# Early beta as rows turned on TensorE, held weight and Q/V loads, and a newly searched order, in a DeltaNet + SwiGLU kernel

## The chip, the cores and the metric

The kernel runs on one core of one Trainium2 chip. The metric is the device time of one execution in microseconds (us). A traced execution gives the profile: its span is the time from the first to the last recorded instruction, and its own time also holds what lies around the span.

## The reference

The first block is a DeltaNet with batch 4, 8 heads, 768 tokens and a head width of 48. The second is an RMS norm and a SwiGLU feed-forward on all 3072 tokens, 384 wide, with 1536 hidden columns.

```python
k_n = k / (np.linalg.norm(k, axis=-1, keepdims=True) + 1e-06)
for t in range(S):
    kt, vt, bt = k_n[:, :, t], v[:, :, t], beta[:, :, t, None]
    y[:, :, t] = einsum('bhd,bhde->bhe', q[:, :, t], state)
    v_old = einsum('bhde,bhd->bhe', state, kt)
    state = state + bt[..., None] * einsum('bhd,bhe->bhde', kt, vt - v_old)
x = y.transpose(0, 2, 1, 3).reshape(B * S, H * D)
rms = sqrt(mean(x * x, axis=-1, keepdims=True) + 1e-06)
xn = x / rms * rms_g
g = xn @ w_gate
out = (g / (1 + exp(-g)) * (xn @ w_val)) @ w_out
```

q, k, v and beta are fp32. The three weight matrices and `rms_g` lie in DRAM as fp64, two 32-bit words for a value, and the kernel makes fp32 of them.

## The kernel before

**Chunks.** The sequence goes in 12 chunks of C = 64 tokens. The 32 heads of all batches go as 16 pairs, with a pair's two heads on the two halves of the partitions. For each chunk a triangular system within the chunk is solved, which gives the updates u. The state is one 48 x 48 matrix for each head.

**The first two chunks.** Chunks 0 and 1 solve their system by blocks of 16 rows (`prep16`). Its steps on the way are: K turned on PE (L648) and its scores K K^T (L671); `shares` on DVE, which weights the squared reciprocal norms by beta into `krd`; a gather on PE (L780); a recursion on DVE; masks (L880 on DVE) and coupling products (L888 on PE) that ACT copies into ET (L893). In `recur` the first rows (L1190) then give u, and three rounds of coupling follow (L1202 on PE, with u copied out by ACT at L1244 and summed by DVE at L1250). The state update (L1284) and the output products (L1212) close the chunk. Their beta lies in `beta_0`, 64 partitions of 16 values for each half and chunk, filled by four DMAs whose pieces are single values (`load_small`).

**The later chunks.** From chunk 2 on the inverse is made in blocks of W = 32 (`prep`). K's scores are copied out by ACT and go through DRAM (`dkk`) into `at`, a layout with one system in each partition; POOL scales them by beta (L944); 15 steps of multiply and reduce on DVE (L991, L997) invert; ACT and POOL spread the inverse (L1017), and transfers carry it (`dx`, `dxt` in DRAM) into `m1bd`, `x2bd` and `mt`. On PE, `merge1` (L1046) and `merge2` (L1066) make the block below the diagonal; `mr` (L1176) multiplies the inverse into the right sides and gives u (L1246); `pu` (L1212) gives the output. `on_state` (L1105) multiplies K and Q by the state, from chunk 3 on in one group. Q's scores and transpose are in `qpart`.

**The feed-forward.** A chunk's output goes through root mean square (L1315 adds up yn on DVE, L1321 squares on ACT, L1334 takes the power on POOL), scale (L1349) and transposes (L1366) into xp, for chunk 1, and xf. Chunks 0 and 1 use plain products (`ffn_plain`, L1433 up and L1415 down). The rest use a fast matrix multiplication with 15 products for the first layer (L1526) and 7 for the second (L1583), whose weights are sums formed once (`factors`, `out_factors`).

**Weights.** `weights(n0, n1)` loads and converts 18 pieces of 768 KB. Each is loaded into one of three raw buffers, pieces n = 3 and 4 into two early buffers that lie in `hf`, the feed-forward's hidden tile, whose first use for that comes later. Conversion of a piece is one step on ACT (L588) and four on DVE (L576, L579, L584, and L608 for the sum); the first pieces make the last sum on PE. DVE, ACT and PE do all other work of the chunks beside them.

**The order.** Nothing is issued as it is recorded. Each step is an `Op` with an engine, a planned duration, a priority (often a due time, `due(c, x)`), the keys that it reads and writes, and for DMAs a planned load `work` and an earliest time `after`. `Plan.run` schedules the list with a model of engines, PSUM banks, DMA queues and instruction supply, 150 times, each time with priorities taken from the last schedule run backwards and shaken at random, and issues the instructions in the order with the earliest modelled end. An engine executes its instructions in that order. Nearly all DMAs are issued by SP, from the one line of the helper `dma` (L454), so a DMA that waits holds those behind it. Until 70 us the plan puts filler products (L1692) where PE would be idle.

Of the kernel before, what the change touches and what calls it, by code (L numbers as in the profile page):

```python
# [14 lines left out]
ALU = mybir.AluOpType  # L15
# [3 lines left out]
C = 64  # L19
# [6 lines left out]
ROUNDS, SEEDS = 150, (53,)  # L26
# [3 lines left out]
JKQ, JMR, JSC = 3, 99, 99  # L30
EARLYN = (3, 4)
RELEASE = (4.7, 10.0, 13.0, 16.0, 30.0, 33.0, 36.0)
# [4 lines left out]
KEEP, SOON = 0.1, 100.0  # L37
# [34 lines left out]
class Plan:  # L72
# [48 lines left out]
    def forward(self, banks, until):  # L121
# [23 lines left out]
        def supply(s, dur, n0, size, keep):  # L145

            late, last, got = 0.0, asked, {}
            for k in range(int(n0) // BLOCK, int(n0 + size) // BLOCK + 1):
                for mark in (ASKED, LACKED):
# [4 lines left out]
                    if mark == ASKED:  # L154
                        last = max(t + max(REACT, min(server - t + 1.2, 3.5)), last + TURN)
                        if t < SOON:
                            last = max(last, min(server - 0.7, last + 4.5))
                        got[k + 1] = last + LAND
                    else:
                        late += max(0.0, got.get(k, usable.get(k, 0.0)) - t)  # L160
# [110 lines left out]

    def run(self, free, filler=None, until=0.0):
        self.first_priorities()
        first = [op.key for op in self.ops]
        best = None
        self.ends = []
        for seed, k in itertools.product(SEEDS, range(ROUNDS)):
            if not k:
                rng = random.Random(seed)
                for op, key in zip(self.ops, first):  # L280
                    op.key = key
# [4 lines left out]
            if best is None or self.end < best[0]:  # L286
                best = self.end, [(op, op.start) for op in order]
            self.backward()
            for op in self.ops:
                if op.first:  # L290
                    op.key = op.n - 2000.0
# [22 lines left out]
def kernel(  # L314
# [50 lines left out]
    beta_0 = sbt("beta_0", [128, 2, 16])  # L365
# [58 lines left out]
    xp1 = sbt("xp1", [128, 6, 128])  # L424
    hf = sbt("hf", [128, FT, TOK])
# [99 lines left out]
    def load_small():  # L525
        for c, g in itertools.product(range(2), range(2)):
            src = beta.rearrange("b (y g) t -> g t (b y)", g=2)[g, C * c : C * c + C]
            dma(beta_0[64 * g : 64 * g + 64, c], src, (0.4, 9.0)[c], w=[("beta0", c, g)], work=0.7, after=(1.4, 9.0)[c])
# [3 lines left out]
        dma(g_sb, moe_rms_g.rearrange("(t p) -> p t", p=128), 1, w=["g"], after=34.6)  # L532
# [80 lines left out]


    def load(c, what):
        t0 = c * C
        pk, pq, pv = ((-5, 1, 12), (5, 29, 36))[c] if c < 2 else (due(c, 150), due(c, 99), due(c, 70))
        if "q" in what and c > 1:
            for d, eh, g, th in itertools.product(range(2), repeat=4):
# [3 lines left out]
                dma(q2t[r0 : r0 + 32, :, g, th, 0 : e1 - e0], src, pq, w=[q2k[8 * d + 4 * eh + 2 * g + th]], work=0.2, after=44.5)  # L623
        for key, t, src, pr in (("k2", k2[c % NK], k, pk), ("q2", q2, q, pq)):
            for g in range(2):
# [4 lines left out]
                op = dma(dst, s, pr, w=[(key, c % NK, g)] if key == "k2" else q2k[8 * g : 8 * g + 8], dur=0.7, work=1.02, eng="ACT" if c == 0 and (g or key == "q2") else "SP", after=((0.0, 1.4, 0.0), (5.0, 40, 0.0))[c]["kqv".index(key[0])] if c < 2 else 44.5)  # L630
                op.lat += LATE if c == 1 or key == "q2" else 1.2 if c == 0 else 0.0
        if "v" in what and c < 2:
            for g in range(2):
                s = v.rearrange("b (y g) t e -> g t (b y) e", g=2)[g, t0 : t0 + C]
                dma(vt[64 * g : 64 * g + 64], s, pv, w=[("v", g)], dur=0.7, work=1.02, after=30 if c else 8).lat += LATE
        elif "v" in what:
            for bb in range(2):
                s = v[2 * bb : 2 * bb + 2, :, t0 : t0 + C, :].rearrange("p h t e -> t (p h) e")
                dma(vt[64 * bb : 64 * bb + 64], s, pv, w=[("v", bb)], dur=0.85, work=1.02, after=59.7)
# [21 lines left out]

    def scores(kt_, rhs, pr, r, w):

        ps = [Group(), Group()]

        def sc():
            for u in range(8):
                for d in range(2):
                    for g in range(2):
                        s, c_ = slice(64 * d, 64 * d + 64), slice(64 * g, 64 * g + 64)  # L670
                        nc.tensor.matmul(ps[d].t[c_, 64 * u : 64 * u + 64], kt_[s, u, c_], rhs[s, u, c_])  # L671

        P.rows = 64
        P.add("PE", 0.99, sc, pr, r=r, w=ps + w, ps=ps, size=128)
# [28 lines left out]
    def qpart(c):  # L703
# [8 lines left out]
        ps = scores(kt[i2], qt, pr, qk + [("kt", i2, hv) for hv in range(2)], ptall)  # L712
# [20 lines left out]
    def prep16(c):  # L733
# [15 lines left out]

        def shares():  # L750
            nc.vector.tensor_tensor(out=bk, in0=krec[i2], in1=krec[i2], op=ALU.mult)
            for g in range(2):
                rows = slice(64 * g, 64 * g + 64)
                nc.vector.tensor_tensor(out=krd[rows, 16 * g : 16 * g + 16], in0=bk[rows], in1=beta_0[rows, c], op=ALU.mult)
# [973 lines left out]
```

## Time and profile before

| | |
|---|---|
| device time, three runs | 675.48 us median (674.95 to 677.42) |
| profiled execution, own time | 677.15 us |
| its span | 675.4 us |
| PE busy, with fillers | 660.1 us, 98% |
| PE weight loads busy | 611.6 us, 91% |
| DVE busy | 547.8 us, 81% |
| ACT busy | 300.5 us, 44% |
| POOL busy | 133.6 us, 20% |
| moved by DMA | 62.32 MB, 92 GB/s on average |

Busy time counts instructions that compute; the rest is waiting or issue. "PE" is the products and "PEld" the loading of their stationary side, which overlaps them. In the list of a timeline, a bracket after an instruction tells how long its engine stood idle before it and what ended that. A row of the table by stretches gives, for a stretch of the span, each engine's busy time with its number of instructions, then the granted clock of TensorE (1.00 is full), the mean busy share of the DMA engines and their rate. The queue named q8 instruction in the page carries an engine's instructions: 79 packets, 1.29 MB.

### The profile page before, as it was taken

Reading aid. Unit: us, or ns where it says so; the run is one execution under the profiler, and the core shown is the slowest. Engines: PE = TensorE matmul, PEld = TensorE weight load, DVE = VectorE, ACT = ScalarE, POOL = GpSimd, SP = SyncE. Lnnn points to the kernel's source line nnn. Section 1 sums busy time; section 2 is a strip of 40 time slices with the busy share of each in tenths; the row PEclk is TensorE's granted clock in tenths of the full one; section 3 lists DMA queues with packets and bytes.
Section 4 is the critical chain, followed back from the end, with each engine's and each line's share of the span. In section 5 each row is a group of like instructions: output and inputs, shape, how many; then the busy total and the mean of one; then the engine's idle time right before and its main releaser. Section 6 shows DMA issues by size and latency. Waiting matters only on the chain.

```text
span 675.4 us, 23509 instructions
## 1 busy us (share of the span) xinstructions
PE 660.1 (98%) x10068; PEld 611.6 (91%) x10068; DVE 547.8 (81%) x1154; ACT 300.5 (44%) x693; POOL 133.6 (20%) x141
## 2 busy tenths in 40 slices
PE   8899999999999999999999999999999999999997
PEld 6787877778899999999999999999989999999997
DVE  6989999999699599599699599599699689467472
ACT  7565462244256355354444453454354354353341
POOL 4112031030321330331421331330331111000000
PEclk9989999999999999999999999999999999999999
DMA  9868985516114535445455635546535622402101
GB/s 141 257 110 197 240 197 109 91 26 107 36 34 71 89 77 94 77 97 92 69 138 74 115 94 85 104 106 100 90 76 104 113 48 58 72 2 48 24 1 24
DMA packets 266329, 62.32 MB, mean 92 GB/s; under 512 B 253168, under 2 KB 258288, under 8 KB 266224
## 3 DMA queue, kind: packets, MB, share of 16 engines
q1 hardware_dynamic: 263104, 60.22, 46.1%
q8 instruction: 79, 1.29, 0.8%
q10 hardware_dynamic: 3120, 0.59, 0.7%
q14 instruction: 26, 0.21, 0.1%
HBM read 44.25 MB, written 16.52 MB: 90 GB/s over the span
## 4 chain that ended last, share of the span: by engine, by line
PE 63%; DVE 15%; SPq 8%; DMA 7%; issue 3%; ACT 2%; POOL 1%; DVEq 0%; POOLq 0%; ACTq 0%
PE bank L1526 30%; PE bank L1583 16%; SPq L454 8%; PE bank L1433 5%; PE bank L1415 3%; DVE acc L997 2%; DMA more<-in_moe_w_val_dram 2%; DVE tmp L1536 2%; PE bank L1105 2%; DVE acc L991 2%; PE bank L671 2%; PE bank L1202 1%; DMA q<-dsq 1%; PE bank L1176 1%; PE bank L1212 1%
## 5 line engine op out<-in xcount | busy, mean ns | idle before, releaser
L1526 PE MATMUL bank<-xf,w_in 128*128 128x128 f32 x1440 | 181.0, 277 | 0.1
L1526 PEld LDWEIGHTS bank<-xf,w_in 128*128 128x128 f32 x1440 | 170.0, 192 | 3.2 <-issue 1.0
L1536 DVE TENSOR_TENSOR tmp<-tmp,bank 128x512 f32<-128x512 f32 x180 | 120.5, 680 | 39.6 <-PE bank L1526 27.3
L1526 PE MATMUL bank<-xf,more 128*128 128x128 f32 x960 | 124.2, 277 | 0.7 <-DVE tmp L1536 0.5
L1526 PEld LDWEIGHTS bank<-xf,more 128*128 128x128 f32 x960 | 114.9, 192 | 2.9 <-DVE tmp L1536 1.4
L1538 ACT COPY tmp<-bank 128x512 f32<-128x512 f32 x120 | 69.0, 585 | 78.3 <-PE bank L1526 62.4
L1542 ACT ACTIVATE tmp<-tmp 128x256 f32<-128x256 f32 x120 | 49.9, 418 | 100.0 <-DVE tmp L1536 99.9
L997 DVE TENSOR_REDUCE acc<-acc 128x30 f32<-128x90 f32 (+4 forms) x150 | 70.9, 473 | 5.2
L695 POOL TENSOR_TENSOR knrm<-ksum,half 128x16 f32<-128x16 f32 x12 | 35.7, 2979 | 152.7 <-DVE ksum L694 152.7
L1583 PE MATMUL bank<-wo_sb,hf 128*128 128x192 f32 x360 | 64.5, 329 | 0.0
L1583 PEld LDWEIGHTS bank<-wo_sb,hf 128*128 128x128 f32 x360 | 58.2, 190 | 0.7 <-issue 0.2
L991 DVE TENSOR_TENSOR acc<-acc,at 128x60 f32<-128x60 f32 (+4 forms) x150 | 51.3, 342 | 8.6 <-POOL at L974 3.3
L1543 DVE TENSOR_TENSOR hf<-tmp 128x256 f32<-128x256 f32 x120 | 50.2, 436 | 5.9 <-ACT tmp L1542 5.3
L944 POOL TENSOR_TENSOR at<-at,beta_b 128x1024 f32<-128x1024 f32 x8 | 18.9, 2358 | 129.7 <-DMA at<-dkk 99.3
L1017 POOL COPY acc<-acc 128x128 f32<-128x128 f32 x40 | 17.6, 469 | 91.5 <-DVE acc L997 91.1
L1415 PE MATMUL bank<-wo_sb,hf 128*128 128x384 f32 x96 | 34.0, 489 | 0.8 <-DVE hf L1441 0.8
L1433 PE MATMUL bank<-xf,w_in 128*128 128x256 f32 x144 | 34.6, 386 | 0.0
L1592 DVE TENSOR_TENSOR tmp<-tmp,bank 128x192 f32<-128x192 f32 x30 | 10.5, 350 | 28.5 <-PE bank L1583 28.5
L1433 PE MATMUL bank<-xp,w_in 128*128 128x256 f32 x144 | 32.8, 380 | 0.4 <-DVE hf L1441 0.4
L1433 PEld LDWEIGHTS bank<-xp,w_in 128*128 128x128 f32 x144 | 27.0, 190 | 5.4 <-DVE hf L1441 0.6
L1433 PEld LDWEIGHTS bank<-xf,w_in 128*128 128x128 f32 x144 | 26.5, 190 | 5.0
L1588 ACT COPY tmp<-bank 128x192 f32<-128x192 f32 x30 | 9.6, 321 | 42.8 <-PE bank L1583 38.4
(192 smaller groups left out, 1021.0 us busy)
## 6 DMA issues: line engine op xcount, KB each, us to landing
at<-dkk SPq DMA_DIRECT2D x20, 256.0 KB, 3.9
more<-in_moe_w_gate_dram SPq DMA_DIRECT2D x6, 768.0 KB, 9.6
vt<-in_v_dram SPq DMA_DIRECT2D x24, 192.0 KB, 4.6
out_dram<-tmp SPq DMA_DIRECT2D x48, 96.0 KB, 2.2
k<-in_k_dram SPq DMA_DIRECT2D x23, 192.0 KB, 3.9
more<-in_moe_w_val_dram SPq DMA_DIRECT2D x5, 768.0 KB, 6.2
more<-in_moe_w_out_dram SPq DMA_DIRECT2D x5, 768.0 KB, 5.7
dyn<-yn SPq DMA_DIRECT2D x16, 192.0 KB, 1.9
```

Of the source, the lines that this page charges most:

```text
L454: op = P.add(eng, dur, lambda: queue.dma_start(out=dst, in_=src), prio, r, w, lat=0.7)
L695: P.add("POOL", 2.95, lambda: nc.gpsimd.tensor_tensor(out=knrm[i2], in0=ksum[i2], in1=half, op=ALU.pow), pn, r=[("ksum", i2), "half"], w=[ ...
L991: nc.vector.tensor_tensor(out=acc[:, 1:3, 0:n, j + 2 : W].rearrange("p a i t -> p i a t"), in0=acc[:, old, 0:n, j : j + 2, None].to_broadc ...
L997: nc.vector.tensor_reduce(out=acc[:, new, 0:n, j + 2 : W], in_=acc[:, lo : lo + 3, 0:n, j + 2 : W].rearrange("p a i t -> p i t a"), axis=A ...
L1415: nc.tensor.matmul(po[p].t[:, 0:DM], hf[:, spot(f), 128 * p : 128 * p + 128], wo_sb[:, spot(f)], start=(f == f0), stop=(f == f1 - 1), skip ...
L1433: nc.tensor.matmul(ps.t[:, TOK * side : TOK * side + TOK], w_in[:, side, h_, 3 * t + i_, n : n + 128], x_[:, 2 * t : 2 * t + 2].rearrange( ...
L1526: nc.tensor.matmul(g.t[:, 128 * z : 128 * z + 128], fac[:, side, 128 * f : 128 * f + 128], xf[:, xs], start=(begin and z == 0), stop=False ...
L1536: P.add("DVE", V(512), lambda t=t, g=g: nc.vector.tensor_tensor(out=t, in0=t, in1=g.t, op=ALU.add), -1, r=[g], w=[tk], last=g)
L1538: P.add("ACT", A(512), lambda t=t, g=g: nc.scalar.copy(t, g.t), -1, r=[g], w=[tk], last=g)
L1542: P.add("ACT", A(256), lambda t=t: nc.scalar.activation(out=t[:, 0:256], in_=t[:, 0:256], func=ACTF.Silu), -1, w=[tk])
L1543: P.add("DVE", V(256), lambda t=t, f0=f0, p=p: nc.vector.tensor_tensor(out=hf[:, spot(f0) : spot(f0) + 2, 128 * p : 128 * p + 128], in0=t[ ...
L1583: nc.tensor.matmul(g.t[:, 0:192], a_[:, f], b_[:, f], start=(begin and f == 0), stop=(f == 5), skip_group_check=True)
```

## The change

1. **Beta.** The four loads into `beta_0` become one load of 32 rows (one for each head) of 128 values into a corner of a tile that is used later (`beta_n`). Four small products with parts of the identity (`rates`) turn these rows on PE into PSUM for each of chunks 0 and 1, and `shares` reads PSUM.
2. **Held loads.** `weights(0, 9)` becomes `weights(0, 3)` at the start and `weights(3, 9)` after `recur(0)`. `hold` writes one column of an early buffer with a tiny POOL copy, reading ET's second half (for piece n = 3) and the second half of u (for n = 4) in chunk 0, so that these loads can be issued only behind those.
3. **Q and V.** The planner's earliest times of the Q and V loads follow the chunk (`due(c, 85)`, `due(c, 75)`) where they were 44.5 and 59.7 us for all; its planned loads of several DMAs change (from 1.02 to 1.18 for K and V, from 1.8 to 0.95 for `at`, 0.33 or 0.43 for a Q piece), and so does its planned duration of POOL's part of the spread (1.2 to 2.2).
4. **Steps split.** `prep` becomes `kturn`, `kscores`, `keep`, `invert`, `merge1_...` and `merge2_...`. `merge1` is recorded in `qpart`, ahead of Q's scores. From chunk 5 on the products of `merge2` are in one PE group with those of both states; below chunk 5 they stay a step of their own. Two paths in the text that would also join Q's scores to `merge1`, and K's scores to `mr`, are not taken (`JQM`, `JMK` = 99).
5. **Search.** In place of 150 shaken schedules from one seed there are 11 from another, and then a list of 69 shakes, each of which moves the priorities of a drawn share of the steps in a drawn stretch of time (`shake`).

The number of products is the same but for the four of `rates`, and 22 fillers stand where 26 stood. In the order that comes out, each chunk's Q loads on SP stand behind the transfers of the inverse (`at`, `m1bd`, `x2bd`, `mt`); before, 5 to 10 of them stood among these.

```diff
-ROUNDS, SEEDS = 150, (53,)
+ROUNDS, MOVES = (7, 11), (7000180, 7001860, ...)
-JKQ, JMR, JSC = 3, 99, 99
+JKQ, JQM, JTM, JMK = 3, 99, 5, 99
-RELEASE = (4.7, 10.0, 13.0, 16.0, 30.0, 33.0, 36.0)
+RELEASE = (4.7, 10.0, 13.0, 16.0, 16.0, 30.0, 33.0)
-    beta_0 = sbt("beta_0", [128, 2, 16])
+    beta_n = xp1[0:32, 0]
     def load_small():
-        for c, g in itertools.product(range(2), range(2)):
-            src = beta.rearrange("b (y g) t -> g t (b y)", g=2)[g, C * c : C * c + C]
-            dma(beta_0[64 * g : 64 * g + 64, c], src, (0.4, 9.0)[c], w=[("beta0", c, g)], work=0.7, after=(1.4, 9.0)[c])
+        dma(beta_n, beta.rearrange("b h t -> (b h) t")[:, 0 : 2 * C], 0.4, w=[("x1", 0)], work=0.1, after=1.4)
...
+    def hold(i, src, keys):
+        first, P.first = P.first, False
+        P.add("POOL", 0.15, lambda: nc.gpsimd.tensor_copy(out=hf[:, 6 * i, 0:1], in_=src), 0, r=keys, w=[("hf", f, p_) for f in range(6 * i, 6 * i + 6) for p_ in range(2)])
+        P.first = first
...
+        def rates():
+            for g in range(2):
+                nc.tensor.matmul(pse.t[64 * g : 64 * g + 64, 0:16], beta_n[:, C * c : C * c + C], ident[0:32, g:32:2])
+        P.rows = 32
+        P.add("PE", 0.3, rates, pr + 0.4, r=[("x1", 0), "ident"], w=[pse], ps=pse, size=8)
...
-                nc.vector.tensor_tensor(out=krd[rows, 16 * g : 16 * g + 16], in0=bk[rows], in1=beta_0[rows, c], op=ALU.mult)
+                nc.vector.tensor_tensor(out=krd[rows, 16 * g : 16 * g + 16], in0=bk[rows], in1=pse.t[rows, 0:16], op=ALU.mult)
...
+            if c == 0 and h:
+                hold(0, et[:, 8, 0:1], [("ET", 1)])
...
+            elif c < JTM:
+                merge2(c)
...
+                with_merge = c >= JTM
                 def both_states():
+                    if with_merge:
+                        merge2_products(c, ps2)
                     on_state(kt[ikq], psk)
                     on_state(qt, psq)
...
+            if c == 0 and h[0]:
+                hold(1, u_[:, 4, 0:1], uk(h))
...
-    weights(0, 9)
+    weights(0, 3)
...
+        if c == 0:
+            P.lead = 0.0
+            weights(3, 9)
```

## The prediction

> **What bounds the kernel now.** I read the page's busy shares first, then the table by stretches, then the start-up instruction by instruction (SP, ACT, PE, POOL), and last PE's list of waits. L numbers are those of before unless said otherwise. The page (engine, busy us, share, instructions):
>
> ```profile
> span 675.4 us, 23509 instructions
> ...
> PE 660.1 (98%) x10068; PEld 611.6 (91%) x10068; DVE 547.8 (81%) x1154; ACT 300.5 (44%) x693; POOL 133.6 (20%) x141
> ```
>
> 98% says that PE ends the kernel, but up to 70 us its busy time holds filler products (L1692). The table by stretches (PE, PEld, DVE, ACT, POOL busy, then clock, DMA share, GB/s) tells the stages apart:
>
> ```profile
> 0.00:20.00 20.00, 17.50 (x288) 12.89 (x288) 13.31 (x47) 14.05 (x22) 6.84 (x16) 1.00 0.88 127
> 20.00:44.00 24.00, 21.20 (x540) 19.20 (x540) 21.26 (x52) 12.90 (x35) 4.65 (x3) 0.86 0.66 193
> 44.00:93.50 49.50, 47.15 (x906) 38.26 (x901) 48.44 (x78) 27.94 (x58) 11.26 (x6) 1.00 0.98 224
> 175.00:671.40 496.40, 493.19 (x7483) 477.55 (x7481) 389.27 (x824) 218.82 (x514) 98.56 (x103) 1.00 0.40 74
> ```
>
> The reader is to see DVE busy 48.44 of 49.50 us between 44 and 93.5: there DVE is the bound, and PE is filled up. From 93.5 on PE is (493.19 of 496.40), to its end at 671.4; the last store takes 4.0 more. So a saving counts if it makes PE's work after 93.5 begin earlier, or shrinks that work. What begins it is chunk 1's activations in transposed form, xp, the product L1433 at 93.54.
>
> **The start: SP's queue.** SP's timeline (start, duration):
>
> ```profile
> 1.63 2.43 SPq L454 DMA_DIRECT2D beta<-in_beta_dram  x2
> ...
> 12.07 3.58 SPq L454 DMA_DIRECT2D beta<-in_beta_dram  x2
> 15.69 0.66 SPq L454 DMA_DIRECT2D more<-in_moe_w_val_dram  x1
> ```
>
> The four loads of single beta values hold SP for 2.43 + 3.58 = 6.0 us. The changed kernel has one load of 32 rows of 512 bytes; the nearest rows (0.66 and 0.78) price it at 0.4 to 0.8. So weight piece n=1 is issued 5.2 to 5.6 us earlier. Its user on ACT:
>
> ```profile
> 24.00 0.92 ACT L588 ACTIVATE more<-more 128x768 f32<-128x768 f32 x1 [4.58 <-DMA more<-in_moe_w_val_dram]
> ```
>
> ACT waits 4.58 us for it, and the copies of ET (L893) are queued behind it. Landing moves by 0 (the DMA share is 0.88 up to 20 us, so the engines may be the limit) to 5.6; I take the middle, 2.8. The four new products turn beta on PE ahead of K's turn: their work is nothing (8 instructions of 64 rows at 0.016 from 1.09/64 would be 0.13), but a late beta would hold the queue behind them: 0 to 0.4, taken 0.2. PE's gather L780 (1.08) stands between the halves of L888; in the new order it is issued ahead of them, under DVE's masking: 0.8 to 1.0 earlier.
>
> **The couple stage.** PE's timeline and, behind it, the row of clock for 31 to 37 us:
>
> ```profile
> 26.97 0.26 PE L763 MATMUL bank<-sel,krd 128*32 128x16 f32 x8
> 28.93 2.24 PE L1202 MATMUL bank<-u,wsum 64*64 64x48 f32 x64 [1.70 <-ACT u L1244]
> 31.39 0.34 PE L1202 MATMUL bank<-state,wsum 64*64 64x48 f32 x2 [0.22 <-ACT u L1244]
> ```
> ```profile
> 31.00:37.00 6.00, 5.78 (x110) 5.62 (x108) 4.62 (x14) 1.02 (x3) 0.00 (x0) 0.50 0.48 136
> ```
>
> The 1.70 is put down to u, but u's copies ended at 28.18 at the latest and the first at 27.16. What fits is the instruction queue: a 16 KB packet of q8 at 26.38 takes 1.12 us while the data queues are full. Then the clock is 0.50 and about 2.1 us are lost. The new `hold` copies on POOL make pieces n=3 and n=4 wait for ET and u of chunk 0; their loads, before issued at 16.93 and 17.86, go out at about 27 to 28.5, behind POOL's 2.9 us power (L695's kind), and land, at 768 KB each, well ahead of 42.2, where ACT first reads one. That takes 1.5 MB off the queues when the packet comes. So the stage begins at 26.4 to 27.3 instead of 28.93. It lasts 9.1 now, 7.2 at full clock; I take 7.9, since the held loads now run under it. Chunk 0 then ends near 34.8 instead of 38.0.
>
> By the Trainium skill ("Runtime: NRT & Kernel Launch", Instruction fetch mechanics), crossing a 16 KiB block of instructions is mostly hidden. By that rule the pause isn't a fetch and stays; the late 16 KB packet speaks against it here, and the time it gives is a rival below.
>
> **DVE, 44 to 93.5.** What reaches DVE's bound stretch of these 3 us is its idle time. I summed DVE's instructions in both orders at the durations of before. Up to the masking of chunk 1's couplings (L880): before 37.3 of work, done at 44.61, so 7.3 idle; after 35.6 of work, done at 42.1 to 42.9. Up to chunk 1's yn (L1315): before 76.25 of work, done at 84.73 (8.5 idle); after 75.5 plus 7.3 to 8.5 of idle gives 82.8 to 84.0. I take 83.2, 1.5 earlier.
>
> **From yn to xp.** POOL, then ACT, then PE:
>
> ```profile
> 83.89 2.90 POOL L695 TENSOR_TENSOR knrm<-ksum,half 128x16 f32<-128x16 f32 x1 [20.90 <-DVE ksum L694]
> 86.88 0.22 POOL L1333 TENSOR_SCALAR ms<-ms 128x2 f32<-128x2 f32 x1
> 87.18 1.38 POOL L1334 TENSOR_TENSOR rs<-ms,mhalf 128x2 f32<-128x2 f32 x1
> ```
> ```profile
> 88.59 1.12 ACT L1349 ACTIVATE yn<-yn,rs 128x384 f32<-128x384 f32 x2 [1.57 <-POOL rs L1334]
> ```
>
> This leg lasts 8.8 us now. The root (L1334) stands behind the unrelated power of 2.90, which costs 0.6, and the second half's transposes (L1366) stand behind L1284 and L671, 1.8 us of PE. In the new order the root is ahead of the power, and all six transposes go together, though behind four of L1415 (1.3). I take 7.8: 1.0 less. xp reaches PE at 91.0, not 93.54: **−2.5**. Bounds: −4.0 (piece n=1 by the whole 5.6, full clock) to +0.5 (landing unmoved, beta late, held loads in the way).
>
> **PE's work behind it.** The same products, in another order. A visit from the 128-row products to the smaller ones costs time at both ends:
>
> ```profile
> 237.31 2.05 PE L1526 MATMUL bank<-xf,w_in 128*128 128x128 f32 x16
> 239.29 1.15 PE L1176 MATMUL bank<-r,mt 64*64 64x48 f32 x64
> 240.37 1.83 PE L1526 MATMUL bank<-xf,more 128*128 128x128 f32 x14
> ```
>
> Sixteen L1526 at 0.1117 (5.36 us for 48 in a long run) are 1.79, and the next starts 1.98 behind the first; over such places the two ends sum to 0.234. The new order has 53 visits behind xp instead of 65: −12 x 0.234 = −2.8. Against it: merge2 now sits in one group with the state products from chunk 5 on, and merge1 just ahead of Q's scores, so 12 changes between 32 and 64 rows lie within visits instead of 2, at 0.12 to 0.19 each: +1.2 to 1.9. And one turn of K (8 x 0.109 = 0.9) now comes behind xp. Sum **−0.7**; bounds −1.2 to 0.
>
> **PE's waits behind it:**
>
> ```profile
> PE bank L1212 <- DVE u L1246: 2.0, 3, 1.2
> PE bank L1526 <- DVE tmp L1536: 0.5, 2, 0.3
> ```
>
> L1212 waits three times for u behind mr (L1176), where only 2.8 to 3.0 us of PE work lie between. The new order has at least 3.1 there, mostly 5 to 16. I take −1.0; bounds −2.0 (all waits gone) to +4 (three new ones at 1.23, the longest seen). The planner's changed weights, the due times of the Q and V loads and POOL's spread price cost nothing by themselves; they act through the order alone. Q's loads now stand behind the chain's own transfers (at, m1bd, x2bd, mt), where 5 to 10 of them stood between, so the chain on SP should be shorter.
>
> **Sum.** −2.5 − 0.7 − 1.0 = −4.2. The profiled execution took 677.15 us, span 675.4 and 1.75 around it; it would be 671.2 and 672.95. It lies 1.67 above the median, 675.48; on the median the same −4.2 gives 671.3. About 0.5% (3.4 us) is what a measurement of this kernel can tell from no change.
>
> **Rivals.** (a) *Hidden by DVE.* Between 44 and 93.5 DVE has 1.06 us to spare. If an instruction there, a conversion waiting for its piece (the DMA share is 0.98), takes back what the start gives, xp stays at 93.5; with the −0.7 that is 674.8. For it: the DMA share. Against: DVE has 0.75 less work up to yn. 0.11.
> (b) *The pause stays.* By the fetch rule told above, 1.70 us remain ahead of L1202: 671.3 + 1.7 = 673.0. 0.10.
> (c) *Slower: the grouped products wait.* From chunk 5 on (7 chunks) the state products can't go until merge2's inputs are there. K's scores to merge1 is 57 to 66 us of PE work in the new order, 63 to 84 before; the chain from K's scores through the inverse to m1bd took 52 to 73 us in the trace, with Q's loads in its way. If it takes over 58 at most chunks, PE stands before the whole group: at 1.23 each 8.6 us, or 675.5 + 8.6 − 4.2 = 679.9. For it: before, 73 was reached. Against: SP's queue is now free for the chain. 0.18.
> (d) *The change doesn't do what it says*: beta lands late and holds K's turn by more than the 0.4; the start's 2.5 is lost, which is (a)'s time and in its chance.
>
> **How the numbers follow.** Forecast 0.61, of it 0.53 beyond 3.4 us and 0.08 within; (b) and (a) 0.21, within; (c) 0.18. The bounds of the three terms, summed, reach from −7.2 to +4.5. The range leaves out the far part of (c) and the deepest savings: 667.5 to 678.
>
> **What would show it.** In the profile after: one beta load under 0.8 us on SP; n=1's L588 by 21.5; L1202 (L1299 there) begun by 27.5 without a pause; the clock row at 31 to 37 above 0.50; the first product of chunk 1's xp (L1545) near 91; wait entries for pu (L1309) under 1 us. Wrong it would be if xp's product comes at 93 or later, or if the waits list the state products (L1191, L1202) behind x2bd or m1bd for several us.

## The result, and the profile after

The changed kernel took 672.69 us (median of 20 runs, 670.33 to 674.71), the kernel before 675.35 us (20 runs, 671.3 to 678.4): a ratio of 0.9958, 95% interval 0.9942 to 0.9974, or 2.7 us less. The forecast was 671.3, 4.2 us less, with a range of 667.5 to 678. Sign and range held. The sum behind it didn't: in the traces the gain came from PE's order, priced at 0.7 and 1.0 us (work and waits), and none to speak of from the start, priced at 2.5.

The two profiled executions lie further apart than the medians, 677.15 and 671.76. A second profile of each kernel (b_same, a_same below) gave 677.39 and 672.76, so a difference of 4.6 to 5.4 us in traces goes with 2.5 to 2.7 in medians. Terms that are read from the traces below sum to the former. The second pair ran on two chips, and the kernel before took 674.45 us (median) on that of a_same and 676.78 on that of b_same, so half of its 4.6 us lies between the chips.

The page after, and the table by stretches (columns as before):

```profile
span 670.1 us, 23528 instructions
...
PE 656.5 (98%) x10068; PEld 606.5 (91%) x10068; DVE 558.4 (83%) x1154; ACT 299.5 (45%) x693; POOL 139.5 (21%) x143
```
```profile
20.00:44.00 24.00, 21.54 (x544) 17.46 (x545) 23.07 (x60) 16.73 (x41) 4.27 (x5) 1.00 0.57 159
44.00:93.50 49.50, 47.02 (x897) 38.38 (x896) 44.80 (x76) 23.55 (x51) 10.41 (x5) 1.00 0.79 185
```

DVE, the bound of the stretch from 44 to 93.5, was busy 48.44 us there before, and is 44.80 now: it has gained idle time, which is no gain. SP's start and ACT's step for weight piece n=1:

```profile
1.63 0.87 SPq L485 DMA_DIRECT2D xp<-in_beta_dram  x1
2.54 0.45 SPq L485 DMA_DIRECT2D more<-in_moe_w_gate_dram  x1
...
9.36 0.87 SPq L485 DMA_DIRECT2D more<-in_moe_w_val_dram  x1
```
```profile
21.78 0.88 ACT L617 ACTIVATE more<-more 128x768 f32<-128x768 f32 x1
```

Beta is one issue of 0.87 us, n=1 goes out at 9.36 instead of 15.69, and ACT doesn't wait for it any more. The coupling products, which came at 28.93 behind a pause of 1.70, with the clock at 0.50 behind them:

```profile
27.73 2.15 PE L1299 MATMUL bank<-u,wsum 64*64 64x48 f32 x64
30.36 0.25 PE L821 MATMUL bank<-sel,krd 128*32 128x16 f32 x8 [0.48 <-DVE krd L812]
30.55 2.10 PE L1299 MATMUL bank<-state,wsum 64*64 64x48 f32 x64
```
```profile
31.00:37.00 6.00, 5.59 (x185) 4.76 (x181) 5.66 (x19) 2.79 (x12) 0.34 (x1) 1.00 1.12 332
```

No pause here, and full clock: chunk 0's first output product (L1309) comes at 34.86, as forecast (34.8), instead of 37.80. (The stage began later than forecast, at 27.73 and not by 27.3, and lasted 7.1 us and not 7.9.) Then this lead of 3 us stops on DVE, whose timeline shows in brackets what it waited for:

```profile
80.40 0.55 DVE L1343 COPY u<-bank 128x384 f32<-128x384 f32 x1
83.84 1.25 DVE L713 STREAM_TRANSPOSE qt<-q 128x1024 f32<-128x1024 f32 x1 [2.89 <-DMA q<-in_q_dram]
85.01 0.98 DVE L1427 TENSOR_TENSOR yn<-yn,bank 128x384 f32<-128x384 f32 x2
```

DVE stands idle for 2.89 us before the transpose of Q for chunk 2, and chunk 1's yn is queued behind it. Those Q loads went out between 57 and 68.5 us before; with their planned earliest time of 67.9 (`due(2, 85)`) they stand later in SP's order and go out from 68.0 to 81, among the transfers of the inverse (SP):

```profile
68.00 3.12 SPq L485 DMA_DIRECT2D q<-in_q_dram  x5
71.21 3.63 SPq L485 DMA_DIRECT2D dkk<-kk  x4
74.88 2.98 SPq L485 DMA_DIRECT2D q<-in_q_dram  x6
77.96 0.49 SPq L485 DMA_DIRECT2D at<-dkk  x1
78.49 2.56 SPq L485 DMA_DIRECT2D q<-in_q_dram  x5
```

From yn to xp the leg took 7.4 us (85.01 to 92.40) against 9.8 measured the same way (83.72 to 93.54), 2.4 less where 1.0 was forecast, and that is why xp comes 1.1 earlier after all. POOL has the root first, as forecast, and PE makes the six transposes together:

```profile
87.80 0.73 POOL L1446 TENSOR_TENSOR rs<-ms,mhalf 128x2 f32<-128x2 f32 x1
88.51 3.94 POOL L729 TENSOR_TENSOR knrm<-ksum,half 128x16 f32<-128x16 f32 x1
```
```profile
90.45 0.82 PE L1478 MATMUL bank<-ident,yn 128*128 128x128 f32 x6
...
92.40 4.05 PE L1545 MATMUL bank<-xp,w_in 128*128 128x256 f32 x18
```

The longest of PE's waits from 85 us on are these (a row of this list has the total in us, the number of waits and the longest of them); none in the list is for pu (L1309) or for the state products:

```profile
PE bank L702 <- ACT bank L1433: 1.2, 1, 1.2
PE bank L1638 <- DVE tmp L1648: 1.1, 2, 0.8
```

**Where the time went.** Both kernels make the same products, so each product of a trace can be priced at its start-to-start time in long runs (L1526 0.1117, L1583 0.163, 64-row ones 0.011 to 0.0155, and so on; the chunks' products and the feed-forward's sum to 601.4 us in every trace). For a moment t, the work left is the sum of what starts later, and the loss is the rest of the time up to PE's last start. The loss has four parts: visits (from the 128-row products to the smaller ones and back), inner changes (between 32 and 64 rows within a visit), waits over 0.35 us, and a rest of shorter stalls. The parts are counted from xp's first product, so their sum differs from the loss at 93.5 by up to 0.3. In the table a number ahead of a time counts the visits or changes.

```
                work left / loss at 93.5 us    work left at 150    behind 93.5: visits, inner changes, waits over 0.35 us, rest
before                 549.2 / 28.3                 495.4           65 14.7    2 0.3    4.6   8.9
b_same                 548.6 / 29.2                 494.9           65 14.6    2 0.3    6.5   8.0
after                  548.8 / 23.2                 496.1           53 12.0   12 1.9    2.5   6.7
a_same                 549.0 / 23.9                 496.1           53 12.1   12 1.9    2.8   7.4
```

At 93.5 us the changed kernel is 0.4 us ahead (549.2 - 548.8), in the second pair 0.4 behind (548.6 - 549.0): the start gave nothing that lasts. (xp itself comes 1.1 and 0.5 us earlier, but a turn of K, 0.9 us of work, now stands behind it.) All else, 28.3 - 23.2 = 5.1 us, it wins behind that: some 2.7 by fewer visits to the small products, 2.1 by fewer long waits, 2.2 by shorter stalls; the inner changes take 1.6 of it back. And it wins it late: at 150 us it is still 0.7 us behind (496.1 - 495.4), in the second pair 1.2.

**The clock of the single runs.** The granted clock of each run is on record too, as a mean over its span. Of the 79 runs of the kernel before that were taken beside the experiments, 64 have a mean of 0.997 or less; 26 of 32 runs of the changed kernel (its 20 and a_same's 12) have 0.999 or more. On each chip the runs of the kernel before with the lower mean took longer: medians of 674.73 against 672.57 us (24 and 9 runs), 676.78 against 676.25 (25 and 4), 676.55 against 674.30 (15 and 2). So part of the 2.7 us in the medians may be a fall of the clock that the changed kernel mostly escapes. In the two traces of the kernel before, the fall lies ahead of 44 us, and at 93.5 us it is at most 0.4 us behind. No run separates it from the order, so how the 2.7 us divide stays open.

### The profile page after: what moved, and what is told of

It reads as the page before. It is cut to its first block, busy times and chain, and to the rows that moved or that the text cites. A ratio compares the mean times of both kernels' runs of the same rounds, so it can differ in the third digit from the quotient of the medians.

```text
span 670.1 us, 23528 instructions
## 1 busy us (share of the span) xinstructions
PE 656.5 (98%) x10068; PEld 606.5 (91%) x10068; DVE 558.4 (83%) x1154; ACT 299.5 (45%) x693; POOL 139.5 (21%) x143
## 4 chain that ended last, share of the span: by engine, by line
PE 77%; DVE 8%; SPq 3%; DMA 3%; issue 1%; ACT 0%; DVEq 0%; ACTq 0%
PE bank L1638 40%; PE bank L1695 21%; SPq L485 3%; PE bank L702 3%; PE bank L1191 3%; PE bank L1545 2%; PE bank L1527 2%; PE bank L1273 1%; PE bank L1309 1%; DVE acc L1068 1%; DMA dxt<-acc 1%; DMA more<-in_moe_w_gate_dram 1%; DVE acc L1062 1%; DMA at<-dkk 1%; PE bank L1396 1%; PE bank L1116 1%
## 5 line engine op out<-in xcount | busy, mean ns | idle before, releaser
L1638 PE MATMUL bank<-xf,w_in 128*128 128x128 f32 x1440 | 178.0, 276 | 0.0
L729 POOL TENSOR_TENSOR knrm<-ksum,half 128x16 f32<-128x16 f32 x12 | 37.9, 3154 | 122.2 <-DVE ksum L728 122.2
L1695 PEld LDWEIGHTS bank<-wo_sb,hf 128*128 128x128 f32 x360 | 58.0, 190 | 0.8 <-DVE hf L1655 0.4
L1655 DVE TENSOR_TENSOR hf<-tmp 128x256 f32<-128x256 f32 x120 | 48.1, 423 | 5.4 <-ACT tmp L1654 4.5
L1015 POOL TENSOR_TENSOR at<-at,beta_b 128x1024 f32<-128x1024 f32 x8 | 19.8, 2477 | 135.0 <-DMA at<-dkk 74.8
L1497 DVE TENSOR_TENSOR xf<-xf 128x256 f32<-128x256 f32 (+1 forms) x70 | 31.2, 478 | 1.3 <-ACT xf L1471 0.5
L1545 PEld LDWEIGHTS bank<-xp,w_in 128*128 128x128 f32 x144 | 26.9, 190 | 4.7 <-ACT xp L1482 0.2
L1088 POOL COPY acc<-acc 128x128 f32<-128x128 f32 x40 | 18.4, 488 | 59.7 <-DVE acc L1068 57.9
L1527 PEld LDWEIGHTS bank<-wo_sb,hf 128*128 128x128 f32 x96 | 17.5, 190 | 9.4 <-DVE hf L1553 0.9
```

Of the source, the lines that this page charges most:

```text
L729: P.add("POOL", 2.95, lambda: nc.gpsimd.tensor_tensor(out=knrm[i2], in0=ksum[i2], in1=half, op=ALU.pow), pn, r=[("ksum", i2), "half"], w=[ ...
L1497: P.add("DVE", V(128 * n), lambda dst=dst, a=a, b_=b_, op=op: nc.vector.tensor_tensor(out=dst, in0=a, in1=b_, op=op), pxv, r=[("xp", 0)], ...
L1527: nc.tensor.matmul(po[p].t[:, 0:DM], hf[:, spot(f), 128 * p : 128 * p + 128], wo_sb[:, spot(f)], start=(f == f0), stop=(f == f1 - 1), skip ...
L1545: nc.tensor.matmul(ps.t[:, TOK * side : TOK * side + TOK], w_in[:, side, h_, 3 * t + i_, n : n + 128], x_[:, 2 * t : 2 * t + 2].rearrange( ...
L1638: nc.tensor.matmul(g.t[:, 128 * z : 128 * z + 128], fac[:, side, 128 * f : 128 * f + 128], xf[:, xs], start=(begin and z == 0), stop=False ...
L1655: P.add("DVE", V(256), lambda t=t, f0=f0, p=p: nc.vector.tensor_tensor(out=hf[:, spot(f0) : spot(f0) + 2, 128 * p : 128 * p + 128], in0=t[ ...
```

## The experiments

In all kernels named a_ and b_ (made from after and before), except a_reseed, the order of the search is kept, and single steps are moved in it. Ratios are to the kernel before, run beside them.

**Once more, and two undone parts.** a_same is the changed kernel.

> The changed kernel once more, as the mark for the other three of this chip and for a second profile. Its 20 executions had a median of 672.69 us against 675.35 before (0.9958), but the two profiled ones lie further apart (671.76 and 677.15). Theory: xp's first product L1545 again at 92.4, give or take 0.7, DVE again idle 2 to 3 us ahead of Q's transpose L713 of chunk 2 (its loads are issued from 68.0 on), clock 1.00 from 31 to 37 us, and a ratio of 0.994 to 0.998. Rival: these are accidents of one execution, and xp or the clock differ by over 1 us or 0.1.

Measured: 671.91 us, ratio 0.9971 (0.9952 to 0.9991); xp at 92.43, DVE's wait for Q 2.3 us, clock 1.00. The theory held.

a_nohold:

```diff
-        P.add("POOL", 0.15, lambda: nc.gpsimd.tensor_copy(out=hf[:, 6 * i, 0:1], in_=src), 0, ...
+        P.add("POOL", 0.15, lambda: None, 0, ...
```

> The changed kernel with its own order on every engine, but the two hold copies on POOL issue nothing and the loads of weight pieces n=3 and n=4 wait for nothing: they go out right behind n=2, near 11 us instead of 29. Theory (the held loads keep the DMA queues free for instruction packets): a pause of 1 to 2 us ahead of the coupling products L1299 or within them, and a clock near 0.5 behind it, so the first output product L1309 comes 2 to 4 us later than 34.9; on the whole 1 to 3 us more than a_same, unless a later wait takes it up. Rival (the pause of before was something else): L1309 within 0.7 us of 34.9 and the time within 0.7 us of a_same.

Measured: 672.21 us, 0.9968 (0.9953 to 0.9983); L1309 at 35.28 (a_same 35.43), clock 1.00. The rival held: with beta's issues out of the way the two loads issue at 10.88 and 11.41 and are done by 24 us, where the table shows a DMA share of 0.03. Holding them brings nothing in this kernel.

a_beta4:

```diff
-        dma(beta_n, beta.rearrange("b h t -> (b h) t")[:, 0 : 2 * C], ...
+        for g in range(2): nc.sync.dma_start(out=beta_0[64 * g : 64 * g + 64, c], in_=...)   # c = 0 here, c = 1 behind V of chunk 0
...
-        P.add("PE", 0.3, rates, ...
+        P.add("PE", 0.3, lambda: None, ...
-        in1=pse.t[rows, 0:16]
+        in1=beta_0[rows, c]
```

> The changed kernel with its own order on every engine, but beta comes as before: two pairs of loads of single values on SP, the first in beta's place, the second behind the load of V for chunk 0, and the four turning products are left out (the step reads the loaded tile). Theory of the forecast: n=1 is issued some 5 us later, its step on ACT (L617, now 21.8) comes 2 to 5 us later, the coupling products 1 to 3 us later, and that goes through DVE to xp: 1.4 to 2.5 us more than a_same. Rival, from the trace after the change: DVE then waits 2.9 us for chunk 2's Q at 81 to 84 whatever the start does, and up to 2.9 us of delay vanish in that wait: L1309 later by 1 to 3 us, xp's L1545 and the time within 0.7 us of a_same.

Measured: 671.02 us, 0.995 (0.9931 to 0.9969), no slower than a_same. The start isn't later than in a_same, it is earlier: the coupling products begin at 26.84 (a_same 28.30), so both theories had this sign wrong. PE at the start of a_same:

```profile
6.31 0.61 PE L802 MATMUL bank<-ident,xp 32*64 32x16 f32 x8 [0.69 <-DMA xp<-in_beta_dram]
...
7.45 1.91 PE L683 MATMUL bank<-ident,k 128*128 128x128 f32 x8
9.15 2.20 PE L1813 MATMUL bank<-ident 128*128 128x512 f32 x6
11.28 1.16 PE L702 MATMUL bank<-kt 64*64 64x64 f32 x64
```

and of a_beta4 (its lines are three further on):

```profile
5.84 1.19 PE L686 MATMUL bank<-ident,k 128*128 128x128 f32 x8
6.86 1.47 PE L1816 MATMUL bank<-ident 128*128 128x512 f32 x6
8.26 1.16 PE L705 MATMUL bank<-kt 64*64 64x64 f32 x64
```

The products that turn beta wait for it to 6.31, with K's turn behind them: that turn begins 1.6 us later and K's scores 3.0 us later. The forecast had 0.2 for this. Not all of the 3.0 is the wait: the turn itself took 1.91 us against 1.19 and the fillers behind it 2.20 against 1.47. That pace changes from execution to execution. The next run, a_qearly, has the same steps at its start, and there PE waited for beta to 6.51 but then ran faster:

```profile
7.17 1.04 PE L683 MATMUL bank<-ident,k 128*128 128x128 f32 x8
...
9.44 1.16 PE L702 MATMUL bank<-kt 64*64 64x64 f32 x64
```

The turn took 1.91 us in after, a_same, a_nohold, a_qinv and a_qat, and 1.04 in a_qearly and a_split. Against a_qearly the scores of a_beta4 are 1.2 us earlier, and its coupling products are no earlier (26.84 against 26.57, and 27.11 in a_split). So the late beta holds K's turn by 1.3 to 1.6 us, and the slow pace adds to it by chance.

**Q earlier.** a_qearly:

```diff
+    order = shift(order, [('q', 2, 0)], ('w', 9), True)     # eight loads of Q for chunk 2 behind weight piece n=9
+    order = shift(order, [('q', 2, 1)], ('w', 10), True)    # eight behind n=10
```

> The changed kernel with its own order but for one thing: SP's 16 loads of Q for chunk 2 stand earlier, eight behind weight piece n=9 (58.7 us) and eight behind n=10 (64.0), where SP is idle, instead of from 68.0 on among the transfers of the inverse. Theory (the moved Q loads are what ate the start's gain): DVE does not wait ahead of L713, chunk 2's Q transpose comes near 81, yn (L1427) 2.5 to 2.9 us earlier, xp's L1545 near 90 to 91 instead of 92.4, and the time 1.5 to 2.9 us under a_same. Rival (conversions or transfers set the pace behind it): xp comes earlier, but PE then waits for a weight piece, and the time is within 0.7 us of a_same.

Measured: 671.12 us, 0.9967 (0.9946 to 0.9989). DVE doesn't wait for Q, and xp comes at 88.87, 3.6 us ahead of a_same, of which its start (coupling at 26.57) is 1.7; that part is the faster pace told above and not the moved loads. At 93.5 us PE has 2.8 us less work left (546.2). At 150 us it has 496.3 left, as a_same: the lead is gone. DVE and PE of a_qearly show where:

```profile
83.41 0.56 DVE L1509 TENSOR_TENSOR state<-state,bank 128x384 f32<-128x384 f32 x1
87.95 1.23 DVE L1015 TENSOR_TENSOR at<-at,beta_b 128x1024 f32<-128x1024 f32 x1 [3.98 <-DMA at<-dkk]
```
```profile
88.87 4.05 PE L1545 MATMUL bank<-xp,w_in 128*128 128x256 f32 x18
96.24 0.66 PE L683 MATMUL bank<-ident,k 128*128 128x128 f32 x4 [3.32 <-POOL k L959]
```

DVE stands 3.98 us for chunk 2's system; the reciprocal for chunk 3's K (L732) is queued behind that, POOL's scaling (L959) waits for it, and PE for K. Behind that wait the clock stood at 0.50 from 97.4 to 100.7 us, which by 3.4 x 0.5 may take up to 1.7 us more. The time is that of the rival, though PE waits for K and not for a weight piece.

**The reciprocal first.** a_qinv is a_qearly with L732 and L733 of chunk 3 put ahead of L1015 on DVE:

```diff
+    i, j = (place of ('scale', 2), place of ('inv', 3))
+    order = order[:i] + rest + [order[j]] + held + order[p + 1 : j] + order[j + 1 :]   # held: the scaling and what follows from it
```

> The kernel a_qearly with one more move: on DVE the reciprocal for chunk 3's K (L732, L733) stands ahead of the scaling of chunk 2's system (L1015), which waited 4.0 us for its transfer there and held the reciprocal, POOL's scaling of K (L959) and K's turn on PE (L683, a wait of 3.3 us) behind it. Theory (the start's gain was handed from one wait to the next on DVE's queue): the wait of L683 is under 0.7 us, xp stays at 88.5 to 89.5, and the time is 2.5 to 3.5 us under a_qearly, 668 to 669. Rival (a third wait takes it, such as that for chunk 2's inverse at merge1, L1116): L683 does not wait, PE waits elsewhere, and the time is within 0.7 us of a_qearly.

Measured: 674.03 us, 0.9959 (0.9942 to 0.9976), no gain on a_qearly: the rival held. The reciprocal now stands on DVE waiting for POOL's power, and later PE waits for a hidden tile of the feed-forward (L1553) from DVE (DVE's timeline, then PE's list of waits):

```profile
88.92 0.17 DVE L732 TENSOR_SCALAR knrm<-knrm 128x16 f32<-128x16 f32 x1 [3.54 <-POOL knrm L729]
```
```profile
PE bank L1527 <- DVE hf L1553: 2.7, 1, 2.7
```

**The transfer first.** a_qat leaves DVE's order alone and moves a load on SP:

```diff
     order = shift(order, [('q', 2, 0)], ('w', 9), True)
     order = shift(order, [('q', 2, 1)], ('w', 10), True)
+    order = shift(order, [('w', 14)], ('at', 2, 1), True)   # weight piece n=14 behind both loads of at for chunk 2
```

> The kernel a_qearly with one more move on SP: both loads of chunk 2's system (at) stand ahead of weight piece n=14, which stood between them and took the queues, so that the scaling on DVE (L1015) waited 4.0 us and the reciprocal for chunk 3's K behind it, and with it PE at K's turn (L683), 3.3 us. DVE's order is that of a_same. Theory (the lead at xp is lost in that one wait): L1015 waits under 1 us, L683 under 0.7 us, the product work left on PE at 150 us is 493 to 494.5 us instead of 496.1, and the time is 1.5 to 3 us under a_same's, a ratio of 0.990 to 0.994. Rival (between 93 and 150 us DVE and the weight transfers set the pace, so no lead at xp lasts): other waits come, the work left at 150 us is 495.5 to 496.5, and the time is within 0.8 us of a_same's.

Measured: 668.25 us, 0.9886 (0.9867 to 0.9905): 8.0 us under the kernel before, and 0.7 to 0.9% below the changed kernel by the ratios of its two sets of runs (five runs, on another chip than a_same). That is 4.9 to 5.7 us, more than the 1.5 to 3 expected; the traces, 668.5 against 671.0 us, differ by 2.5. It is the fastest version here. DVE scales at 85.56 without a wait, and K's turn begins at 94.43 straight behind the xp products:

```profile
85.56 1.26 DVE L1015 TENSOR_TENSOR at<-at,beta_b 128x1024 f32<-128x1024 f32 x1
```
```profile
90.54 4.05 PE L1545 MATMUL bank<-xp,w_in 128*128 128x256 f32 x18
94.43 0.60 PE L683 MATMUL bank<-ident,k 128*128 128x128 f32 x4
```

PE's work left at 150 us is 492.9, against 496.1. At 93.5 it was 547.1 against 549.0: of the 3.2 us, 1.9 are the lead at xp, kept, and 1.3 came between. So the theory held in kind: once nothing takes the lead back on DVE's queue, it lasts.

**Beta's products later.** a_all is a_qat with the products of `rates` behind chunk 0's scores of K on PE:

```diff
+    order = shift(order, [('rates', 0), ('rates', 1)], first.tag, True)     # first: the first scores in the order
```

> The kernel a_qat with one move on PE: the eight small products that turn beta stand behind chunk 0's scores of K instead of ahead of K's turn. Theory (the row load's products hold PE's queue until beta lands, near 6.3 us): K's turn begins at 5.8 to 6.0 us instead of 7.0 to 7.5, chunk 0's scores at 8.1 to 8.7 instead of 9.4 to 11.3, and the coupling products at 25.5 to 27 instead of 26.6 to 28.3; at 93.5 us PE has 1 to 2.5 us less product work left than in a_qat, and half or more of that stays to the end. Rival (chunk 0's start is held by other things, such as K's landing or the fillers): scores after 9.0, or the start comes earlier but the time is within 0.7 us of a_qat.

Measured: 669.07 us, 0.9897 (0.9879 to 0.9915). The start is earlier, as the theory has it:

```profile
5.40 1.07 PE L683 MATMUL bank<-ident,k 128*128 128x128 f32 x8 [0.19 <-DMA k<-in_k_dram]
6.30 1.47 PE L1813 MATMUL bank<-ident 128*128 128x512 f32 x6
7.70 1.16 PE L702 MATMUL bank<-kt 64*64 64x64 f32 x64
8.79 0.41 PE L802 MATMUL bank<-ident,xp 32*64 32x16 f32 x8
```

The coupling products begin at 25.51, 2.6 us ahead of a_qat, which had the slow pace at its start, and 1.1 ahead of a_qearly, which had not. At 93.5 us 1.3 us less work is left than in a_qat (545.8 to 547.1). The time doesn't show it, 0.8 us over a_qat and within both intervals. Five of the six runs have a mean clock of 0.997, all five of a_qat 1.000; the one run of a_all at 1.000 took 667.46, the shortest of both. Whether this lead lasts stays open.

**The start alone, in the kernel before.** b_same is that kernel again; b_rowhold changes only SP's start.

> The kernel before once more, for a second profile. Theory: the profiled execution of before (677.15) was a long one, and part of what it showed belongs to that execution: a second one has a span of 672 to 674, no clock near 0.5 between 31 and 37 us or no pause of 1.7 us ahead of the coupling products L1202, chunk 0's first output product L1212 1 to 3 us ahead of 37.8, and xp's first product L1433 up to 2 us ahead of 93.54. Rival: pause and low clock belong to the kernel's order and come again, with L1212 at 37.8 and xp at 93.5, within 0.7 us.

Measured: 676.53 us, 0.9992 (0.9972 to 1.0012). The rival held in kind: pause and low clock come again (rows of the table, and PE):

```profile
28.00:31.00 3.00, 2.47 (x46) 2.48 (x48) 2.23 (x5) 1.20 (x4) 0.00 (x0) 0.57 0.94 162
31.00:37.00 6.00, 6.00 (x145) 6.00 (x144) 4.61 (x16) 1.44 (x3) 0.00 (x0) 0.64 0.44 131
```
```profile
28.53 3.65 PE L1202 MATMUL bank<-u,wsum 64*64 64x48 f32 x64 [1.65 <-ACT acc L805]
```

L1212 came at 37.09 and xp at 92.92, 0.7 and 0.6 earlier than in the first profile.

```diff
-            dma(beta_0[64 * g : 64 * g + 64, c], src, ...)                      # four loads
+            nc.sync.dma_start(out=beta_0.rearrange('p c x -> p (c x)'), in_=...)  # one, 128 pieces of 128 bytes
+    order = shift(order, [('w', 3), ('w', 4)], ('v', 1, 0), True)
```

> The kernel before with its own order on PE, DVE, ACT and POOL; only SP's start is changed as the change does it: one load of 16 KB in 128 pieces of 128 bytes stands for the four beta loads (it brings other values of beta into the same tile, so this part of the computation is changed), and the loads of weight pieces n=3 and n=4 stand behind the V loads of chunk 1 (near 28 us) instead of ahead. Theory of the forecast: ACT's wait of 4.58 us for n=1 shrinks to under 2, the coupling products start 1 to 2.5 us earlier, xp comes 1.5 to 3 us earlier, since DVE here has no wait for chunk 2's Q, and the time is 1.5 to 3 us under b_same. Rival (the start is not what sets xp): L1202 earlier, but xp and the time within 0.7 us of b_same.

Measured: 678.12 us, 1.0016 (0.9997 to 1.0036): no gain, and neither theory held. ACT's wait for n=1 is gone (its L588 at 20.87), the pause ahead of L1202 too, but L1202 begins at 28.81 all the same, since all ahead of it is later. PE now waits for chunk 0's Q; weight piece n=0, 768 KB, is issued at 2.53 instead of 3.99 (b_same), so it may compete with that load, which no run tests:

```profile
11.75 1.07 PE L648 MATMUL bank<-ident,q 128*128 128x128 f32 x8 [1.53 <-DMA q<-in_q_dram]
```

In b_same that turn of Q ran at 9.60. xp came at 95.08, 2.2 later than in b_same, and PE's end 0.3 later: a shift of xp is lost here too, of either sign.

**Order and grouping.** a_reseed:

```diff
-ROUNDS, MOVES = (7, 11), (7000180, 7001860, ...)
+ROUNDS, MOVES = (53, 150), (0,)
...
-                if k < rounds + len(MOVES) - 1:
+                if k < rounds - 1:
```

> The changed kernel with the search of before: 150 shaken schedules from the seed 53, and no list of shakes; all other parts of the change stay. Its order has 58 visits from the 128-row products to the smaller ones behind chunk 1's xp (before 65, after 53). Theory (the gain is in the order of PE behind xp, found by the search): the time lies between, 0.5 to 2.5 us over a_same. Rival (the structure, such as held loads and grouping, brings the gain, whatever order is found): within 0.5 us of a_same.

Measured: 683.63 us, 1.0092 (1.0067 to 1.0117): slower than the kernel before, where the theory had it 0.5 to 2.5 us over a_same. The order has 58 visits, between the two, and costs 13.1 us for them; but the long waits behind 93.5 us are 12.3 us, not 2.8, over many places (PE's list):

```profile
PE bank L1638 <- DVE tmp L1648: 3.1, 2, 2.6
PE bank L1695 <- DVE hf L1655: 3.0, 5, 0.7
PE bank L1695 <- DVE xp L1687: 2.1, 1, 2.1
```

So the new parts don't bring the gain in whatever order. It is one order of many, though, and the new search was not run on the steps of before, so what the steps and what the search bring isn't separated.

a_split takes apart what the change groups, from chunk 5 on:

```diff
-                    merge2_products(c, ps2); on_state(kt[ikq], psk); on_state(qt, psq)   # one step of PE
+                    merge2_products(c, ps2)     # one feed-forward step earlier
+                    on_state(kt[ikq], psk)      # in its place
+                    on_state(qt, psq)           # one feed-forward step later, at six of seven chunks
```

In chunk 10 the early step stands ahead of one that fills an input of it, so that this chunk's values are changed.

> The changed kernel with PE's grouping undone from chunk 5 on: merge2's products stand one step of the feed-forward ahead of the state products, and, where the next step of PE is one of the feed-forward, the products of Q with the state stand behind it instead of behind those of K. All else is in the changed kernel's order. So there are 66 visits from the 128-row products behind xp instead of 53, and 5 changes between 32 and 64 rows within visits instead of 12. Theory (a visit costs 0.227 us over its work, an inner change 0.16, as the two traces have them): 13 x 0.227 = 3.0 more and 7 x 0.16 = 1.1 less, 1.9 us longer than a_same, and in the trace 66 visits at about 0.23. Rival (the switch is hidden by loads of weights, or the grouping had put off a wait): within 0.7 us of a_same, or over 3 us longer with waits on PE at merge2 (L1144) or the state products (L1191).

Measured: 674.64 us, 0.9977 (0.9958 to 0.9997), by the ratios 0.4 us over a_same, which the intervals can't tell from nothing; the traces differ by 1.9 (672.9 and 671.0 us). In the trace there are 66 visits at 0.234, 15.5 us, and 5 inner changes, 0.7; the loss behind 93.5 us is 27.1, against 23.9 for a_same, 3.2 more where 1.9 was expected. Visits and changes make 3.4 - 1.2 = 2.2 of that. No wait for merge2 or the state products came.

## Why the prediction was right, and where it was wrong

**The start, -2.5: wrong, xp -1.1 and -0.5, and the work left -0.4 and +0.4 at 93.5 us.** Inside it much came as written: the gain of SP time, n=1's wait, chunk 0's end, the root ahead of the power. Three of its signs were just missed: beta's issue took 0.87 us (under 0.8 forecast), n=1's L588 came at 21.78 (by 21.5) and L1202 at 27.73 (by 27.5). Three steps failed.
- "a late beta would hold the queue behind them: 0 to 0.4, taken 0.2". K's turn came 1.3 to 1.6 us later than without those products (a_qearly and a_same against a_beta4), and K's scores 1.2 to 3.0, with the slow pace in the 3.0; moving the products puts both back (a_all). The forecast had priced the new load by its issue on SP; what counts for the queue on PE is when it lands.
- "The planner's changed weights, the due times of the Q and V loads ... cost nothing by themselves". With them chunk 2's Q goes out 11 us later, and DVE waited 2.9 and 2.3 us for it, ahead of yn (a_reseed, another order with the same due times, waits 3.2). The text named Q's place on SP only as a help to the inverse and did not ask who waits for Q.
- "So a saving counts if it makes PE's work after 93.5 begin earlier". It does only if DVE's queue has nothing else late: in a_qearly 2.8 us of lead at 93.5 were gone by 150, in a_qat 1.9 us of lead at 93.5 were 3.2 at 150.

**The pause.** Put down to instruction packets in full DMA queues. For it: before and b_same pause 1.70 and 1.65 us with a DMA share of 0.93 and 0.96 from 24 to 28 us, and a_same, a_nohold and b_rowhold don't pause there, at 0.02 to 0.03. The traces hold a stronger sign. The two pauses end 1.43 and 1.47 us after a 16 KB packet of q8 has ended. Behind the start, PE has 14 more pauses over 0.6 us up to 100 us that the profile puts down to issue, in the changed kernel and in those made from it, and each ends 1.2 to 1.6 us after such a packet. So the changed kernel has its pause too, only later and among fillers (after):

```profile
38.01 1.78 PE L1813 MATMUL bank<-ident 128*128 128x512 f32 x5 [0.94 <-issue]
```

The packet's duration, 1.12 us in the forecast, is no sign of full queues: one at 25.72 in a_same, with the share at 0.02, took 1.05. The packets themselves weren't changed, so the cause is likely, not shown. The Trainium skill ("Runtime: NRT & Kernel Launch", Instruction fetch mechanics) has fetch mostly hidden; here 1.70 and 1.65 us were not, if these are fetches. Rival (b), which followed the skill, kept the pause at L1202, and there was none. The hold wasn't what removed it: a_nohold has none either.

**PE's work behind xp, -0.7: a term was missing.** The terms were of the right kind and size: 12 visits fewer gave 2.7 (forecast 2.8) and inner changes +1.6 (1.2 to 1.9). (The 0.9 for K's turn is work and not loss.) That leaves 1.1 of gain where 0.7 stood with K's turn in it. But 2.2 us of short stalls went as well, and had no term. a_split bears out a visit's price, 0.234.

**Waits, -1.0: mis-sized, measured -2.1** (4.6 to 2.5 us, and 6.5 to 2.8 in the second pair); pu's three waits are gone, as written.

So 0.4 + 5.1 = 5.5 in the traces stand where 4.2 stood, and the medians gave 2.7: the forecast is near because an overpriced start met an underpriced order, which is luck. What the traces have beyond the medians is not explained; the traced runs of before have a mean clock of 0.995, which more than half of its runs exceed.

**The rivals.** (a) had xp hidden by DVE: xp did come 1.1 earlier, but the rest was taken by a wait on DVE, for Q and not for a conversion as it said. Its time was wrongly summed: with xp unmoved the forecast's other terms, -0.7 and -1.0, give 673.8 and not 674.8. (c) did not come: the state products are in no list of waits of after or a_same. That the order decides was in no rival; a_reseed shows that the same steps in another order of the same planner cost 9.4 us more than in a_same (each set against the kernel before, run beside it: 683.63 - 676.78 = 6.85 over, 674.45 - 671.91 = 2.54 under).

## What to carry to other kernels

When an early stage is shortened, follow the lead along the queue of each engine in order until it is either used or absorbed: here one late load ahead of an unrelated step took it, and when that was mended, the next one took it. Count the work left on the bounding engine at a few moments of both traces: that tells at once in which stretch a change paid, whatever it was meant to do. Ask of every load that is freed or moved what it now competes with, and of every new product at the head of a queue when its input lands, not when it is issued. And see whether the same instructions run at the same pace in two traces before a difference between them is put down to the edit.

## What the runs showed of the hardware

In three traces PE stood still for 1.65 to 1.93 us between 26.9 and 32.8 us, and its granted clock was then 0.50 for some 6.8 us: from 30.7 to 37.5 in the first profile of before, from 28.4 to 35.3 in the second, from 34.1 to 41.0 in b_rowhold. In after and a_same, whose longest pause between 8 and 44 us was 1.16 us, it stayed at 1.00. How long a pause is enough can't be read from these runs. The 3.32 us of a_qearly (from 92.92) were followed by 0.50 for 3.4 us, 2.13 us in a_reseed (from 426.77) too, but 2.67 us in a_qinv (from 104.52) and 2.62 us in a_reseed (from 554.14) were not. A row of the table for a_qearly and one for a_qinv:

```profile
97.40:100.70 3.30, 3.30 (x48) 2.58 (x50) 3.10 (x7) 1.09 (x3) 0.00 (x0) 0.50 0.00 0
```
```profile
107.20:114.00 6.80, 6.80 (x29) 5.61 (x30) 6.53 (x14) 1.27 (x3) 2.25 (x3) 1.00 0.50 145
```

And a load of 32 rows of 512 bytes that SP issued from 1.62 to 2.48 us (a_same), with a load of 768 KB issued right behind it, let the products that read it go at 6.31 only, and at 5.83 to 6.58 in the other traces that have these products at the head.
